# Loading v together with the cast of q and k in an attention and feed-forward kernel, with measured DMA times in its build-time plan

## The chip, the cores and the metric

One core of a Trainium2 chip. The metric is the device time of one execution in microseconds (us), the median of several runs. A profile's span (first to last instruction) is about 1.7 us shorter than the time of the same run. A run that lies more than 1.5% above the fastest of its kernel is called slow here and is left out of every ratio. Ratios are the mean time of one kernel's fast runs over the mean of the kernel before's fast runs of the same rounds, so they are not quite the ratios of the medians that are quoted; each comes with a 95% interval.

## The reference, cut to what matters

```python
# q, k, v: (8 batches, 8 heads, 576 positions, 64)
scores = scale * q @ k.T
# heads 0-3: causal band of 32 positions; heads 4-7: every 4th of the last 128
attn = softmax(where(mask[h], scores, -1e9))
x = (attn @ v)  ->  (4608 tokens, 512)
h = x @ w_in                       # 512 -> 2048
out = (h * sigmoid(h)) @ w_out     # 2048 -> 512
```

## The kernel before

Tokens go through the two layers in nine groups of 512. Layer 1 and layer 2 are 1152 matmuls of 128x512 in all. Batches 0 and 1 get q and k transposed by PE. Batches 2 to 7 take another way, all by DMA:

- **cast(b)**: q and k are copied in DRAM from float32 to float16 (`kq_s`), issued by POOL.
- **turn(b)**: four DMA transposes, issued by SP, bring `kq_s` into SBUF as `nat` and `kqT`.
- **v(b)**: three loads of v with a cast, issued by POOL, into `vraw` and `vp` (two buffers).
- Scores, exp, mask, AV product; x goes to DRAM (`x_s`) by four stores on SP's queue, and one more DMA transpose on SP's queue brings group b back as `xA` or `xR`.

Every engine's queue runs in order. What order the instructions stand in is decided while the program is built, by a small plan in the Python code: it keeps a clock for PE, holds expected durations for everything else, and always picks a step that it believes to be ready. If a date in the plan is too early, the engine stands before a semaphore on the chip, with useful work behind it in its queue.

```python
    class Plan:
        def push(self, step, gen, ready):
            self.now = ready
            ...eng, us = next(gen)...            # runs the code up to the next yield
        def flush(self):
            while self.heap and self.heap[0][0] <= self.t:
                ready, _, step, gen, eng, us = heapq.heappop(self.heap)
                if eng == "DMA":
                    self.push(step, gen, ready + us)
                    continue
    ...
    def count(key, n, then):                     # an event that waits for n others
        counts[key] = counts.get(key, 0) + 1
        if counts[key] == n:
            then()

    def turn_gen(b):
        issue_turn(b)
        yield "DMA", 9.0
        count(("L", b), 3 if b >= 2 * PEB else 2, lambda: start_loads(b))   # PEB = 2

    def loads_gen(b):
        for i in range(2):    # POOL waits here for the transposes of turn(b)
            nc.gpsimd.tensor_copy(fence[:, i : i + 1], kqTs[b % 2][:, i, 1, HN * M - 1 :])
        if b >= 2 * PEB:      # ... and here for the x transpose of group b - 2
            nc.gpsimd.tensor_copy(fence[:, 2:3], x_of(b - 2)[:, HP - 1, GT - 1 :])
        issue_v(b)
        if b + 1 < B:
            issue_cast(b + 1)
        yield "DMA", 7.0
        v_in[b].done = plan.now
        yield "DMA", 6.0
        if b + 1 < B:
            count(("T", b + 1), 2, lambda: start_turn(b + 1))

    def first_cast():                            # cast(2) is issued in the prologue
        yield "DMA", 52.0
        count(("T", PEB), 2, lambda: start_turn(PEB))
```

`turn(b)` waits for two events: cast(b) has landed, and the scores of batch b-2 are placed. `loads(b)` waits for turn(b), for the AV products of batch b-2 and, from batch 4 on, for group b-2.

The softmax here doesn't subtract the row's maximum and nothing guards it: scores larger than these inputs give would overflow.

## Time and profile before

| | before |
|---|---|
| time, median of 3 runs | 371.25 us |
| span of the profiled run | 368.1 us |
| PE busy | 307.8 us, 84% |
| granted TensorE clock, mean | 0.94 |

The first page of the profile, of before. The line PE gives the busy tenths in 40 equal slices of the span (9.2 us each), PEclk the granted clock, DMA the busy share of the 16 DMA engines.

```profile
span 368.1 us, 5678 instructions
PE   0588999299933999499808999999999999999995
PEclk9999999779975999879957999999999999999999
DMA  8999998999995997999998964127100100100112
```

PE is dense from about 195 us on. Before that, and after the start, there are four dents (66, 104, 151 and 182 us), each with a lower granted clock in it or right behind it, while the DMA engines are busy. The three longest of PE's waits, of before (us in total, times, longest):

```profile
PE h L638 <- DVE gT L649: 13.0, 4, 12.0
PE av_p L472 <- DMA vp<-in_v_dram: 12.7, 2, 7.0
PE h L638 <- DMA xA<-x_s: 12.5, 1, 12.5
```

PE's instructions in order of time show where they are. The columns are start, duration, engine, line, tiles, form, count, and in brackets the idle time before and what ended it:

```profile
65.81 0.35 PE L436 MATMUL s<-nat 64*128 64x96 f16 x8
73.14 0.38 PE L472 MATMUL av_p<-vp,probs 128*128 128x65 f16 x4 [6.98 <-DMA vp<-in_v_dram]
73.33 1.90 PE L666 MATMUL y<-w_out,gT 128*128 128x512 f16 x4
...
103.96 0.28 PE L472 MATMUL av_p<-vp,probs 128*128 128x65 f16 x4
116.73 1.89 PE L638 MATMUL h<-xA,w_in 128*128 128x512 f16 x4 [12.48 <-DMA xA<-x_s]
...
157.17 0.38 PE L472 MATMUL av_p<-vp,probs 128*128 128x65 f16 x4 [5.67 <-DMA vp<-in_v_dram]
...
194.37 1.86 PE L638 MATMUL h<-xR,w_in 128*128 128x512 f16 x4 [12.01 <-DVE gT L649]
```

The first line pair: the scores of batch 2 could run, the AV product right behind them found no v, and layer 2 (`y<-w_out`), which needed nothing, stood in the queue behind it. Afterwards four layer matmuls take 1.90 us instead of about 1.03: the granted clock is 0.50 from 73.1 to 79.1 us. This is called the cold clock below.

POOL and SP in order of time, of before, show one cycle: cast and v issued together, the turn (SP), the fences behind it, the next v.

```profile
66.05 0.80 POOL L118 DMA_DIRECT2D kq_s<-in_k_dram  x1
66.83 0.78 POOL L118 DMA_DIRECT2D kq_s<-in_q_dram  x1
85.74 0.19 POOL L306 COPY fence<-kqT 128x1 f16<-128x1 f16 x1 [17.98 <-DMA kqT<-kq_s]
86.90 0.19 POOL L306 COPY fence<-kqT 128x1 f16<-128x1 f16 x1 [0.97 <-DMA kqT<-kq_s]
87.45 1.34 POOL L141 DMA_DIRECT2D vraw<-in_v_dram  x2 [0.37 <-issue]
```

```profile
75.98 5.84 SPq L131 DMA_TRANSPOSE nat<-kq_s  x2
81.87 2.95 SPq L135 DMA_TRANSPOSE kqT<-kq_s  x2
84.93 1.02 SPq L490 DMA_DIRECT2D x_s<-oP  x2
```

Cast 3 was through at 75.98, when the transposes of turn 3 started. They had landed at 86.9, and only then did v of batch 3 leave. SP was taken up for 8.8 us with issuing them, and a store stood behind them.

### The profile page before, as it was taken

What the parts mean: (1) busy time and instruction counts of PE and PEld (TensorE: products, weight loads), DVE (VectorE), ACT (ScalarE), POOL (GpSimd) and SP (SyncE); (2) the same over time, 40 slices, a digit from 0 to 9 for tenths busy, and PEclk for the clock granted to TensorE, in tenths of its full rate; (3) what the DMA queues carried; (4) which work ended last, traced back from release to release, by engine and by line L of the source; (5) the groups of instructions that cost most, each with busy time, mean ns of one, the idle gap of its engine ahead of it and who ended that gap; (6) DMA issues with size and microseconds to landing.
All of it is one profiled execution on the core that took longest, in us unless ns stands there. A gap on an engine that the chain in (4) does not pass through costs nothing.

```text
span 368.1 us, 5678 instructions
## 1 busy us (share of the span) xinstructions
PE 307.8 (84%) x2200; PEld 149.1 (41%) x2200; DVE 198.8 (54%) x477; ACT 153.8 (42%) x258; POOL 48.9 (13%) x80
## 2 busy tenths in 40 slices
PE   0588999299933999499808999999999999999995
PEld 0563545144411444244303444544444444444442
DVE  5694779268940887369404785585345245245200
ACT  1554772036621554435303545445345245245211
POOL 8634001305002200400400300000000000000000
PEclk9999999779975999879957999999999999999999
DMA  8999998999995997999998964127100100100112
GB/s 111 189 203 201 191 199 160 160 214 159 192 195 118 190 241 175 149 190 209 144 216 188 150 89 103 47 90 129 61 28 28 59 28 28 59 29 28 59 62 81
DMA packets 115899, 47.42 MB, mean 129 GB/s; under 512 B 82592, under 2 KB 111264, under 8 KB 115872
## 3 DMA queue, kind: packets, MB, share of 16 engines
q0 software_dynamic: 47152, 19.92, 44.0%
q1 hardware_dynamic: 63536, 17.70, 25.7%
q10 hardware_dynamic: 5184, 9.44, 7.0%
q8 instruction: 17, 0.28, 0.3%
q14 instruction: 10, 0.08, 0.1%
HBM read 39.84 MB, written 20.05 MB: 163 GB/s over the span
## 4 chain that ended last, share of the span: by engine, by line
PE 64%; DMA 22%; POOL 4%; DVE 3%; SPq 2%; issue 2%; ACT 2%; ACTq 0%; POOLq 0%
PE y L666 30%; PE h L638 29%; DMA vp<-in_v_dram 4%; DMA w_out<-in_moe_w_out_dram 4%; DMA xR<-x_s 3%; DMA w_in<-in_moe_w_in_dram 3%; DMA kq_s<-in_k_dram 2%; PE s L436 2%; DMA x_s<-oD 2%; SPq L131 1%; PE av_p L472 1%; DMA nat<-kq_s 1%; POOL vraw L141 1%; PE av_d L472 1%; DMA xA<-x_s 1%
## 5 line engine op out<-in xcount | busy, mean ns | idle before, releaser
L649 DVE SCALAR_TENSOR_TENSOR gT<-th,h 128x512 f16<-128x512 f32 x144 | 97.9, 683 | 86.2 <-ACT th L647 86.0
L666 PE MATMUL y<-w_out,gT 128*128 128x512 f16 x576 | 141.4, 386 | 0.8 <-ACT ob L677 0.7
L647 ACT ACTIVATE th<-h 128x512 f32<-128x512 f32 x144 | 85.9, 597 | 115.4 <-PE h L638 94.3
L638 PE MATMUL h<-xR,w_in 128*128 128x512 f16 x384 | 93.8, 384 | 12.0 <-DVE gT L649 12.0
L638 PEld LDWEIGHTS <-w_in 128*128 128x128 f16 x576 | 54.8, 100 | 89.5 <-issue 22.6
L666 PEld LDWEIGHTS <-gT 128*128 128x128 f16 x576 | 54.5, 99 | 62.2 <-issue 4.3
L638 PE MATMUL h<-xA,w_in 128*128 128x512 f16 x192 | 52.5, 406 | 14.3 <-DMA xA<-x_s 12.5
L677 ACT ACTIVATE ob<-y 128x512 f32<-128x512 f32 x36 | 21.5, 597 | 61.4 <-PE y L666 61.4
L444 ACT ACTIVATE probs<-s 128x768 f16<-128x768 f32 (+2 forms) x45 | 36.4, 810 | 17.6 <-PE s L436 15.5
L472 PEld LDWEIGHTS <-probs 128*128 128x128 f16 x448 | 23.6, 103 | 27.6 <-issue 13.3
L476 DVE TENSOR_TENSOR oD<-av_d,rcps 72x256 f16<-72x256 f32 x64 | 26.9, 420 | 2.2
L472 PE MATMUL av_p<-vp,probs 128*128 128x65 f16 x192 | 13.5, 204 | 14.2 <-DMA vp<-in_v_dram 12.7
L475 DVE RECIPROCAL rcps<-av_p 96x4 f32<-96x4 f32 x48 | 8.3, 173 | 26.2 <-PE av_p L472 26.0
L476 DVE TENSOR_TENSOR oP<-av_p,rcps 96x256 f16<-96x256 f32 x48 | 20.2, 420 | 1.7
L475 DVE RECIPROCAL rcps<-av_d 72x4 f32<-72x4 f32 x64 | 10.9, 171 | 15.7 <-PE av_d L472 15.7
L306 POOL COPY fence<-kqT 128x1 f16<-128x1 f16 x12 | 2.6, 220 | 120.6 <-DMA kqT<-kq_s 120.6
L472 PE MATMUL av_d<-vd,probs 128*128 128x65 f16 x256 | 16.0, 200 | 0.7 <-DVE xA L541 0.3
L451 DVE TENSOR_TENSOR probs<-probs,mask_d 128x864 f16<-128x864 f16 (+1 forms) x24 | 13.2, 550 | 2.7 <-ACT probs L444 2.5
L451 DVE TENSOR_TENSOR probs<-probs,mask_p 128x768 f16<-128x768 f16 x24 | 13.2, 552 | 1.6 <-ACT probs L444 1.4
L406 PE MATMUL td<-ident,nat 96*128 96x96 f16 x48 | 4.3, 242 | 11.1 <-DMA nat<-in_k_dram 6.9
L155 POOL DMA_DIRECT2D vp<-in_v_dram x8 | 11.5, 1439 | 2.2 <-DMA nat<-in_q_dram 2.1
L141 POOL DMA_DIRECT2D vraw<-in_v_dram x16 | 10.8, 677 | 4.3 <-issue 2.0
(62 smaller groups left out, 116.7 us busy)
## 6 DMA issues: line engine op xcount, KB each, us to landing
out_dram<-ob ACTq DMA_DIRECT2D x36, 256.0 KB, 2.4
kq_s<-in_k_dram POOLq DMA_DIRECT2D x6, 576.0 KB, 9.3
kq_s<-in_q_dram POOLq DMA_DIRECT2D x6, 576.0 KB, 11.7
vp<-in_v_dram POOLq DMA_DIRECT2D x7, 384.0 KB, 7.7
w_in<-in_moe_w_in_dram POOLq DMA_DIRECT2D x4, 512.0 KB, 12.0
w_out<-in_moe_w_out_dram POOLq DMA_DIRECT2D x4, 512.0 KB, 16.5
vraw<-in_v_dram POOLq DMA_DIRECT2D x8, 224.0 KB, 5.2
x_s<-oP SPq DMA_DIRECT2D x12, 144.0 KB, 2.2
```

Of the source, the lines that this page charges most:

```text
L141: nc.gpsimd.dma_start(out=vraw[p0 : p0 + m1 - m0, ab].rearrange("p h r d -> p h (r d)"), in_=src[m0:m1],)
L155: nc.gpsimd.dma_start(out=vp[:, j0:, :D], in_=win)
L444: nc.scalar.activation(p2, both[:, :, :n], AF.Exp, scale=scale)
L451: nc.vector.tensor_tensor(p2, p2, mk, ALU.mult)
L472: nc.tensor.matmul(a[:, i, : D + 1], lhs(i), rhs(i), start=True, stop=True)
L475: nc.vector.reciprocal(rcp[:n], a[:n, :, D : D + 1])
L476: nc.vector.tensor_tensor(o, a[:n, :, :D], rcp[:n, :, None].broadcast_to([n, HN, D]), ALU.mult)
L638: nc.tensor.matmul(h, w_in16[:, c, f * P : (f + 1) * P], x_g[:, c], start=(c == 0), stop=(c == HP - 1),)
L647: nc.scalar.activation(th, h, AF.Tanh, scale=0.5)
L649: nc.vector.scalar_tensor_tensor(gTs[g][:, f], th, 1.0, h, ALU.add, ALU.mult)
L666: nc.tensor.matmul(y, gTs[g][:, f, tb * P : (tb + 1) * P], w_out16[:, f], start=(f == 0), stop=(f == NFF - 1),)
L677: nc.scalar.activation(ob, y, AF.Copy, scale=0.5)
```

## The change

The intent: v of a batch leaves together with the cast of the same batch, before its turn, so that v is long there when the scores are done; one batch per cycle; and the plan gets the durations that were measured (turn 12.5 us, v 9.0, cast 4.5 more). The first cast moves out of the prologue, behind v(2). Cut to its core:

```diff
-    issue_cast(2)
...
     def turn_gen(b):
         issue_turn(b)
-        yield "DMA", 9.0
-        count(("L", b), 3 if b >= 2 * PEB else 2, lambda: start_loads(b))
+        yield "DMA", 12.5
+        if b + 1 < B:
+            count(("L", b + 1), loads_need(b + 1), lambda: start_loads(b + 1))
+
+    def loads_need(b):
+        return 3 if b >= 2 * PEB else 2 if b > PEB else 1
...
     def loads_gen(b):
-        for i in range(2):
-            nc.gpsimd.tensor_copy(fence[:, i : i + 1], kqTs[b % 2][:, i, 1, HN * M - 1 :])
+        if b > PEB:
+            for i in range(2):
+                nc.gpsimd.tensor_copy(fence[:, i : i + 1], kqTs[(b - 1) % 2][:, i, 1, HN * M - 1 :])
...
         issue_v(b)
-        if b + 1 < B:
-            issue_cast(b + 1)
-        yield "DMA", 7.0
+        issue_cast(b)
+        yield "DMA", max(9.0, 52.0 - plan.now)
         v_in[b].done = plan.now
-        yield "DMA", 6.0
-        if b + 1 < B:
-            count(("T", b + 1), 2, lambda: start_turn(b + 1))
+        yield "DMA", 4.5
+        count(("T", b), 2, lambda: start_turn(b))
...
-    def first_cast():
-        yield "DMA", 52.0
-        count(("T", PEB), 2, lambda: start_turn(PEB))
```

The two other places that count `("L", b + 2)` now use `loads_need(b + 2)`.

More of the change, by code (lines that the diff above doesn't have):

```diff
@@ L333, in group_gen @@
         if g == b and b + 2 < B:
-            count(("L", b + 2), 3, lambda: start_loads(b + 2))
+            count(("L", b + 2), loads_need(b + 2), lambda: start_loads(b + 2))
     def stored(b):
@@ L622, in attention @@
                             lambda: count(
-                                ("L", b + 2), 3 if b >= PEB else 2, lambda: start_loads(b + 2)
+                                ("L", b + 2), loads_need(b + 2), lambda: start_loads(b + 2)
                             )
@@ L692, in layer2 @@
         return steps
-    plan.push(Step(None, 0.0), first_cast(), 0.0)
     att = []
```

## The prediction

> **What bounds it.** PE is busy 84% of the 368.1 us span, but by ten-microsecond windows it is dense only from 201 us on. Before that (PE lines and waits in order of time) it stands still four times after the first layer-1 matmul at 29.4 us: 66–73 us (7.0, for vp of batch 2), 104–117 (12.5, xA of token group 2), 151–157 (5.7, vp of batch 5), 182–194 (12.0; behind it an ACT queue that waits for the DMA transposes of batch 7). That is 37 us. After each stop the matmuls take twice as long for a while (1.71 instead of 0.86 us for four). The Trainium skill, "TensorE: Matmul & The Clock Gate", Part 1, says an idle PE drops to half rate until about 3.4 us of activity; the trace agrees: some 3 us a stop, 11 in all.
>
> Floor from the trace: 1152 layer matmuls at 0.2165 us = 249, attention of seven batches near 5 us each = 35, 3 for batch 1's transposes, 29.4 lead, 3.5 tail: 320 us. So about 48 us are stops and cold clock.
>
> **Why it stops.** Queues are in order, the order is fixed at build time. The plan counts 9.0 us for a turn (four transposes); the trace shows 10.9 to 12.7. It counts 7 us for v, the trace 9.7. And v(b) is issued only after turn(b) has landed (POOL's fence waits 120.6 us for kqT), so the AV product behind the scores finds no v.
>
> **The change** adds and removes no work: same bytes, a few fences less. cast(2) moves behind v(2). v(b) leaves with cast(b), before turn(b). In the trace v+cast takes 11.0 to 12.7 us to land, the turn as above; the new plan has 13.5 and 12.5, slightly conservative, as it should be.
>
> Estimated course: v(2)+cast(2) land at 54 us (50.2 now, plus 0.77 MB at about 195 GB/s), turn(2) at 66, v(2) long there. No vp stop. Attention takes some 22 us a batch, so batch 2 is stored by 93 and group 2 turned by 98 instead of 116.7. Groups 0 and 1 with attention keep PE busy until about 98: little of the 12.5 us stop stays.
>
> **Its cost.** cast(b) and turn(b) now wait for group b-2 as well. The loop over two batches is load 12 + turn 11.5 + attention 22 + store behind SP's turn issue (up to 9) + x transpose 6 = 55 to 60 us, so 28 to 30 per group, like today's spacing (28 to 31). PE needs about 32 per group (27.7 layers + 5 attention), so it should just stay fed, with small stops from SP's blocked stores, which the plan doesn't know.
>
> **Prediction.** Floor 320, plus 5 to 14 for remaining stops and cold clock, plus 2 from span to time: 334 us (10% less), range 318 to 354. Chances: faster by over 2% 0.88, within 2% 0.07, slower 0.05.
>
> **Signs that it is right:** vp no longer among PE's waits in mid-span; group 2's first layer-1 matmul near 98 us; idle PE after 29 us below 15 us; granted clock mean about 0.97; PE work unchanged; last x transpose earlier than now (255 us).
>
> **What would make it wrong:** cast(2) landing after 60 us behind v(1) and w_out; a loop longer than 33 us per group, so that PE starves at every group; ACT's output DMAs again held behind late transposes; or scores placed early, so that stops move from vp to the transposes.

## The result, and the profile after

| | before | after |
|---|---|---|
| median of 4 runs | 370.88 us | 340.75 us (336.27 to 341.09) |
| ratio, 95% interval | 1 | 0.9154 (0.9073 to 0.9235) |
| span of the profiled run | 368.1 us | 339.4 us |
| PE busy | 307.8 us | 304.1 us |
| mean granted clock | 0.94 | 0.985 |

The first page, of after, and PE's longest waits, of after (those of the first 29 us are left out):

```profile
span 339.4 us, 5670 instructions
PE   0678998999999883999999999599999999999995
PEclk9999999999999997999999999879999999999999
DMA  8999999899759995995699989972260100200121
```

```profile
PE h L636 <- DMA xR<-x_s: 6.0, 1, 6.0
PE s L434 <- DMA nat<-kq_s: 3.6, 1, 3.6
PE h L636 <- DVE gT L647: 2.6, 5, 0.8
```

The vp wait is gone, and of four dents two are left, near 130 and 215 us. PE in order of time, of after:

```profile
73.62 0.35 PE L434 MATMUL s<-nat 64*128 64x96 f16 x8
...
103.92 1.02 PE L636 MATMUL h<-xA,w_in 128*128 128x512 f16 x4
...
124.63 1.89 PE L636 MATMUL h<-xA,w_in 128*128 128x512 f16 x8
132.49 3.28 PE L636 MATMUL h<-xR,w_in 128*128 128x512 f16 x8 [5.97 <-DMA xR<-x_s]
...
218.38 0.51 PE L434 MATMUL s<-nat 64*128 64x96 f16 x8 [3.59 <-DMA nat<-kq_s]
```

Batch 2's first scores stand at 73.6 us, and PE runs through the place where it stood for v. Group 2 starts at 103.9 instead of 116.7. Then group 3 is late (132.5). SP in order of time, of after, shows what it waited behind:

```profile
109.25 0.86 SPq L507 DMA_DIRECT2D x_s<-oD  x1
115.03 6.91 SPq L131 DMA_TRANSPOSE nat<-kq_s  x2
122.04 2.72 SPq L135 DMA_TRANSPOSE kqT<-kq_s  x2
124.85 0.85 SPq L507 DMA_DIRECT2D x_s<-oD  x1
127.77 2.53 SPq L326 DMA_TRANSPOSE xR<-x_s  x1
```

The last store of batch 3 had its data at 114.47 us (DVE wrote `oD` there) and was issued at 124.85, behind the four transposes of turn 4. The x transpose of group 3 could only follow.

**Reading the plan against the chip.** The plan's own dates can be printed while the program is built, and each step's date compared with the start of the same matmuls in the trace: the 2200 PE matmuls of the trace answer the plan's steps one to one. The difference is the chip's lag behind the plan. It grows mainly where PE stands still or runs cold (a few lines, in us):

```
                           before              after
                           plan  chip  lag     plan  chip  lag
group 0, layer 1           26.1  29.4   3.2    26.1  28.8   2.7
batch 2, first scores      58.0  62.8   4.9    69.3  73.6   4.4
batch 2, first AV product  60.9  73.1  12.3    72.6  76.9   4.2
group 2, layer 1           90.0 116.7  26.8   100.3 103.9   3.6
group 3, layer 1          121.9 150.2  28.3   123.2 132.5   9.3
batch 5, first AV product 123.1 157.2  34.0   149.8 160.5  10.7
batch 6, first scores     147.4 196.2  48.8   184.6 195.3  10.8
batch 7, first scores     178.5 228.3  49.7   204.1 218.4  14.3
group 8, layer 1          273.7 322.5  48.9   277.3 293.8  16.5
```

So the new plan itself ends 3.6 us later than the old one (319.0 against 315.4 us). All the gain, and more, is that the chip keeps up with it: the lag fell from 48.9 to 16.5 us. In every kernel of this case the span was the plan's end plus the lag at group 8 plus 3.8 to 4.0 us. (The plan's end is its last step's end. The expectations of runs 1 to 8 below give the start of that step, 0.9 us earlier.)

The printed dates also show *what* was false in the old plan. It held turn 2 for landed at 28.8 us and v of batch 2 at 30.9; on the chip it was 62.8 and 73.0. No duration of 9 or 7 us explains that. The cause is `count`. The code after a `yield` runs as soon as the wait *begins*, with the clock of the event set to its *end* (cast 2: 52 us). `count` drops that date: `then()` starts at the date of whoever is counted last, and for turn 2 that was the placing of the scores of batch 0, at 19.8 us. The changed kernel has the same `count`, but there loads(2) waits for one event alone, and for turn 2 the late event happens to be counted last. Its plan for batch 2 is therefore true (69.0); for loads(3) it is false again (59.4, while the turn that it waits for ends at 69.0 in the same plan).

### The profile page after: what moved, and what is told of

Same layout as the page of the kernel before. It is cut to its first block, busy times and chain, and to the rows that moved or that the text cites. A ratio compares the mean times of both kernels' runs of the same rounds, so it can differ in the third digit from the quotient of the medians.

```text
span 339.4 us, 5670 instructions
## 1 busy us (share of the span) xinstructions
PE 304.1 (90%) x2200; PEld 147.2 (43%) x2200; DVE 200.3 (59%) x477; ACT 154.2 (45%) x258; POOL 49.5 (15%) x78
## 4 chain that ended last, share of the span: by engine, by line
PE 80%; DVE 7%; DMA 6%; ACT 4%; issue 1%; POOL 1%; ACTq 0%; SPq 0%; POOLq 0%
PE y L664 36%; PE h L636 35%; PE s L434 3%; PE av_d L470 2%; DMA nat<-in_q_dram 2%; DVE gT L647 2%; PE av_p L470 2%; ACT th L645 2%; ACT ob L675 1%; DMA xR<-x_s 1%; DMA nat<-kq_s 1%; DVE oD L474 1%; DVE oP L474 1%; PE td L404 1%; DVE probs L449 1%
## 5 line engine op out<-in xcount | busy, mean ns | idle before, releaser
L636 PE MATMUL h<-xR,w_in 128*128 128x512 f16 x384 | 95.7, 388 | 6.1 <-DMA xR<-x_s 6.0
L664 PEld LDWEIGHTS <-gT 128*128 128x128 f16 x576 | 53.2, 98 | 60.8 <-issue 3.0
L636 PE MATMUL h<-xA,w_in 128*128 128x512 f16 x192 | 48.5, 390 | 2.8 <-DVE gT L647 2.6
L442 ACT ACTIVATE probs<-s 128x768 f16<-128x768 f32 (+2 forms) x45 | 36.4, 810 | 22.3 <-PE s L434 19.8
L141 POOL DMA_DIRECT2D vraw<-in_v_dram x16 | 10.8, 677 | 5.1 <-DMA nat<-in_k_dram 2.4
## 6 DMA issues: line engine op xcount, KB each, us to landing
kq_s<-in_q_dram POOLq DMA_DIRECT2D x6, 576.0 KB, 12.5
w_out<-in_moe_w_out_dram POOLq DMA_DIRECT2D x4, 512.0 KB, 16.6
```

Of the source, the lines that this page charges most:

```text
L141: nc.gpsimd.dma_start(out=vraw[p0 : p0 + m1 - m0, ab].rearrange("p h r d -> p h (r d)"), in_=src[m0:m1],)
L442: nc.scalar.activation(p2, both[:, :, :n], AF.Exp, scale=scale)
L636: nc.tensor.matmul(h, w_in16[:, c, f * P : (f + 1) * P], x_g[:, c], start=(c == 0), stop=(c == HP - 1),)
L664: nc.tensor.matmul(y, gTs[g][:, f, tb * P : (tb + 1) * P], w_out16[:, f], start=(f == 0), stop=(f == NFF - 1),)
```

## The experiments

Three theories of the gain: **A**, v leaves before the turn (the order); **A'**, the measured durations; **B**, a plan whose dates are true, whatever the order. Runs 1 to 4 ran on one chip. "Before" was 370.7 us there. The changed kernel was not run again beside the experiments; it is compared with them through its own ratio to before (0.9154), which comes from an earlier session. One run of four was slow in each of runs 3, 8 and 11, two of four in runs 10 and 12.

### 1. The durations alone

```diff
 (kernel before)
-        yield "DMA", 9.0
+        yield "DMA", 12.5
...
-        yield "DMA", 7.0
+        yield "DMA", 9.0
         v_in[b].done = plan.now
-        yield "DMA", 6.0
+        yield "DMA", 4.5
```

> The kernel before with the change's measured times alone (turn 12.5, v 9.0, cast 4.5 us); the order of loads as before. Printed at build, this plan ends layer 2 at 314.5 us and still holds v of batch 2 for landed at 32.9 us (the chip: 73), because an event that waits for several things takes the time of whichever is counted last. Theory A (what pays is that v leaves before the turn): 365 to 372 us, as before. Theory A' (what pays is the measured times): about 341. Theory B (what pays is a plan whose arrivals are true, and the counting is what made it false): 360 to 372, with the vp stop near 66 us still there, some 7 us.

Measured: 365.68 us, ratio 0.9881 (0.9816 to 0.9946). Two of PE's waits of this run:

```profile
PE h L638 <- DMA xA<-x_s: 14.0, 1, 14.0
PE av_p L472 <- DMA vp<-in_v_dram: 11.8, 2, 6.2
```

The stops for v and for group 2 are about as long as before. A' falls. What shrank is the fourth stop: PE's wait `h <- DVE gT`, 13.0 us before, is 5.5 us here.

### 2. The order alone

```diff
 (changed kernel)
-        yield "DMA", 12.5
+        yield "DMA", 9.0
...
-        yield "DMA", max(9.0, 52.0 - plan.now)
+        yield "DMA", max(7.0, 46.0 - plan.now)
         v_in[b].done = plan.now
-        yield "DMA", 4.5
+        yield "DMA", 6.0
```

> The changed order of loads with the old times (turn 9.0, v 7.0, cast 6.0 us; first v at 46, first cast at 52). Theory A (the order pays): 341 to 348 us, no stop for vp. Theory A' (the times pay): 360 to 372. Theory B (true arrivals pay): in between, 345 to 355: the new order has fewer false arrivals, but each turn is planned 2 to 3 us too early, so stops move to the transposes and to the x groups.

Measured: 352.1 us, ratio 0.949 (0.9435 to 0.9545). The stop moved, as B said:

```profile
PE s L434 <- DMA nat<-kq_s: 16.7, 3, 10.8
```

No wait for vp, but 16.7 us for transposes that the plan holds for done after 9 us. (They took 10.9 to 12.7 us in before, so the 9 alone does not explain the longest stop, 10.8 us for batch 7; its other part was not traced.) The order brings 5.1%, and with the durations 8.5%. This edit of the order also changes what `count` gets wrong (turn 2 is dated 61.0 us here, 28.8 in before), so the 5.1% is not the worth of the order alone.

### 3 and 4. The old order with honest counting

```diff
 (kernel before; run 4 has run 1's durations too)
+    latest = {}
     def count(key, n, then):
         counts[key] = counts.get(key, 0) + 1
+        latest[key] = max(latest.get(key, 0.0), plan.now)
         if counts[key] == n:
+            plan.now = latest[key]
             then()
```

> The kernel before with one edit: an event that waits for several things starts at the latest of them, not at the one counted last. Old order, old times. The plan then has turn 2 landed at 61 us, v of batch 2 at 68 (before: 28.8 and 30.9), and ends at 315.0. Theory A (order of v): 365 to 372. Theory A' (the times): 365 to 372. Theory B (true arrivals): 340 to 352, no 7 us stop for vp of batch 2, small stops of 2 to 4 us per batch, since a turn is still planned 2 us too short.

Measured (run 3): 357.43 us, ratio 0.9616 (0.9542 to 0.9691). Faster, but less than B said: the plan gives a cycle of 22 us (turns 2 to 7 landed at 61, 83, 105 and so on), where a cycle of before took 24 us at best, and two stops for vp come back, for batches 5 and 7:

```profile
PE av_p L476 <- DMA vp<-in_v_dram: 17.2, 2, 8.8
```

> The kernel before with the old order of loads, the honest count and the measured times (turn 12.5, v 9.0, cast 4.5). Its plan ends at 319.5 us, against 318.2 for the changed kernel. Theory A (v before the turn is what pays): 360 us or more. Theory B (a true plan pays, in either order): 326 to 340 us, lag of the chip behind the plan below 17 us at the end (before: 49, after: 16.5).

Measured (run 4): 346.54 us, ratio 0.9355 (0.9307 to 0.9402), lag 20.1 us. A falls as the whole explanation: v still leaves after the turn, and 6.5 of the 8.5% are there. B promised a little too much (326 to 340 us, lag below 17). Two of PE's waits of run 4:

```profile
PE h L642 <- DMA xA<-x_s: 5.0, 1, 5.0
PE av_p L476 <- DMA vp<-in_v_dram: 4.0, 1, 4.0
```

The durations were worth 1.2% beside a false count and 2.6 points (0.9616 to 0.9355) beside a true one.

### 5 to 8. What is left: SP's queue, or false dates?

Theory **C**: stores of x stand behind transposes in SP's queue. Theory **D**: the plan's dates for batches 3, 5 and 7 are still false by the count. All four ran on one chip (before: 369.7 us).

```diff
 5 (changed kernel), stores from ACT's queue; both places
-                nc.sync.dma_start(          # x_s <- oP, x_s <- oD
+                nc.scalar.dma_start(
 6 (changed kernel), honest count: the edit of run 3
 7 (run 6), the turn as four steps of the plan
-        issue_turn(b)
-        yield "DMA", 12.5
+        for part in issue_turn(b):          # yields 3.2, 3.2, 1.4, 1.4 after its transposes
+            yield "DMA", part
+        yield "DMA", 3.3
 8 (run 7), and the stores from ACT's queue
```

> The changed kernel with the 24 stores of x issued from ACT's queue instead of SP's; plan unchanged. In the changed kernel SP holds the last store of batch 3 back behind the four transposes of turn 4 (store ready near 114 us, issued 124.85), and the same with batches 5 and 6. Theory C (SP's in-order queue is what is left to gain): group 3 comes about 3 us earlier (its x transpose still stands behind turn 4), as does group 5; 334 to 338 us. Theory D (what is left is that the plan's arrivals for batches 3, 5 and 7 are up to 10 us too early, because of the counting): 339 to 342, nothing gained.

> The changed kernel with the honest count (an event that waits for several things starts at the latest). Its plan ends later, 322.0 us against 318.2. Theory C: SP still holds stores behind transposes: 339 to 344. Theory D (false arrivals are what is left): lag behind the plan at the end falls from 16.5 to 7 to 11 us, the stops for group 3 (6.0 us) and for batch 7's transposes (3.6) go, 333 to 338 us.

> The kernel of the honest count, and a turn issued as four steps in the plan, so that stores and x transposes may stand between its four transposes in SP's queue. The plan's times are the same as with the honest count alone (322.0 us). Theory C: 3 to 6 us faster than the honest count alone. Theory D alone: the same as the honest count alone within 1.5 us, since there the stores are planned after the turn anyway.

> Honest count, turn in four steps and stores from ACT's queue together. If C and D both hold it is the fastest: 328 to 335 us. If ACT waits for the stores' data or for a semaphore of a transpose, it stops instead, as it did near 182 us in the kernel before: 340 us or more.

| run | median us | ratio (95%) | plan's end | lag |
|---|---|---|---|---|
| after | 340.75 | 0.9154 (0.9073–0.9235) | 319.0 | 16.5 |
| 5 stores on ACT | 344.71 | 0.9322 (0.9262–0.9382) | 319.0 | 21.7 |
| 6 honest count | 342.31 | 0.9241 (0.9179–0.9304) | 322.8 | 13.6 |
| 7 and turn in four | 341.25 | 0.921 (0.9145–0.9275) | 322.8 | 15.0 |
| 8 and stores on ACT | 344.87 | 0.9293 (0.9217–0.9369) | 322.8 | 16.6 |

None is faster than the changed kernel, and neither C nor D gets what it promised. Honest counting did lower the lag, by 2.9 us, and made the plan 3.8 us longer. Turning in four halved group 3's stop (2.6 instead of 5.6 us in run 6) and gave it back as a stop of 3.8 us for batch 7's transposes, which now share SP's queue with the stores. With the stores on ACT, group 3 waits 3.4 us (run 5) or nothing (run 8), but ACT, which empties PSUM for PE, is held up: in run 8 its queue stood 13.5 us for `oD`, the data of the stores, and 4.7 us for the transposes `nat<-kq_s` (neither is among its waits in after), as the expectation had warned. PE's two longest waits after the start, of run 8:

```profile
PE h L643 <- DVE gT L654: 10.4, 13, 3.1
PE y L671 <- ACT ob L682: 6.0, 6, 2.2
```

In the profile after these were 2.6 and 1.9 us.

### 9 to 12. The dates of batch 2, the gate of the loads, and a plan without slack

Theory **E**: group 2 came at 103.9 instead of the predicted 98 because the plan dates batch 2's scores late, and all else hangs on it. Theory **F**: the stops only move. One chip (before: 370.8 us).

```diff
  9 (changed kernel)                       10: the same on run 6
-        yield "DMA", max(9.0, 52.0 - plan.now)
+        yield "DMA", max(9.0, 46.0 - plan.now)
 11 (run 10), loads no longer wait for group b-2
-        return 3 if b >= 2 * PEB else 2 if b > PEB else 1
+        return 2 if b > PEB else 1
...
-        if b >= 2 * PEB:
-            nc.gpsimd.tensor_copy(fence[:, 2:3], x_of(b - 2)[:, HP - 1, GT - 1 :])
...
-        b = need[g]
-        if g == b and b + 2 < B:
-            count(("L", b + 2), loads_need(b + 2), lambda: start_loads(b + 2))
 12 (run 7), first v at 46, cast 3.0 instead of 4.5, last yield of the turn 2.1 instead of 3.3
```

> The changed kernel with one number of its plan changed: the first v is expected at 46 us instead of 52 (so cast 2 at 50.5, turn 2 landed at 63 instead of 69). In the changed kernel turn 2 has landed at 66.6 us on the chip, but its scores stand at 73.6, because the plan put them late; group 2 came at 102.4 instead of the predicted 98. Theory E (group 2's late arrival is the mis-sized term, and every later group hangs on it): first scores of batch 2 near 67 us, group 2 near 97, and the whole 4 to 7 us faster than the changed kernel, 333 to 337 us. Theory F (the stops of the chip behind the plan are what is left; they only move): group 2 earlier, but 338 to 343 us.

> The same with the honest count. Plan end 317.9 us (honest count with 52: 322.8; the changed kernel: 319.0). Every span so far was the plan's end plus the final lag of the chip behind it plus 3.9 us. Theory E: lag stays at 13 to 14 as with the honest count, so a span of 335 to 336, time 335 to 338. Theory F: lag grows by what the plan gained, 340 to 343.

> The one before, without the wait of the loads of batch b for the x transpose of group b-2 (it is no data dependence). It tests the predicted cost of the change: that v, cast and turn of a batch now hang on group b-2. If that loop limits the groups, batches 4 to 7 are turned 5 to 10 us earlier, the groups come every 26 us or less, and it is 3 to 8 us faster than the run with the gate. If loads then collide with the stores and transposes of x (DMA saturated), groups come as late as before or later: equal or slower.

> Honest count, first v at 46, cast 3.0 after v instead of 4.5, turn in four steps with 11.3 us in all instead of 12.5: the durations as the trace has them, without slack. Plan end 317.2 us. If slack in the plan costs what it adds, 333 to 337 us. If a plan without slack is caught out by every late landing (as the run with the changed order and the old times was: lag 30.8), 340 to 348 us.

| run | median us | ratio (95%) | plan's end | lag |
|---|---|---|---|---|
| 9 first v at 46 | 341.53 | 0.9239 (0.9197–0.9282) | 317.5 | 17.1 |
| 10 honest, 46 | 340.99 | 0.9143 (0.9082–0.9203) | 317.9 | 16.0 |
| 11 no gate | 354.77 | 0.9549 (0.9475–0.9623) | 318.1 | 34.6 (slow run) |
| 12 no slack, in four | 343.6 | 0.9209 (0.9138–0.928) | 317.2 | 19.7 |

Run 9 is the direct test of E, and E falls. Group 2 starts 5.3 us earlier, at 98.6 us, as had been predicted; group 3 only 1.4 us earlier, and PE's wait for it grew from 6.0 to 8.7 us. PE and then SP in order of time, of run 9:

```profile
131.10 3.37 PE L636 MATMUL h<-xR,w_in 128*128 128x512 f16 x8 [8.65 <-DMA xR<-x_s]
```

```profile
112.16 7.33 SPq L131 DMA_TRANSPOSE nat<-kq_s  x2
119.60 2.94 SPq L135 DMA_TRANSPOSE kqT<-kq_s  x2
122.63 0.85 SPq L507 DMA_DIRECT2D x_s<-oD  x1
126.20 2.77 SPq L326 DMA_TRANSPOSE xR<-x_s  x1
```

The store of batch 3 was ready at 111.3 us (DVE) and again waited for turn 4 to be issued. Run 12, where stores may pass, waits only 0.9 us for groups, but 11.3 us for transposes.

Run 11 says the opposite of what it was made for: without the gate it is slower than run 10 in fast runs (350.75, 354.33 and 355.21 us against 337.22 and 339.58). So the gate, which is no data dependence, pays; why was not shown. One reading is that it keeps the loads apart from the stores and transposes of x. That transfers meet on the DMA engines there fits what the Trainium skill says ("DMA: Bandwidth & Descriptors", "Issuing engines are not separate DMA queues": transfers of all issuing engines run on the same 16 DMA engines and interleave), but the meeting itself was not measured. A rival is SP's queue: other dates also change which stores stand behind which transposes. Its profile fell on the one slow run, so its lines are not shown.

No version is clearly faster than the changed kernel; run 10 (0.9143) ties with it (0.9154).

## Why the prediction was right or wrong

The time (334 predicted, 340.75 measured) lies in the range and the direction is right. Point by point:

- **"PE stands still four times ... 37 us": right; "some 3 us a stop" of cold clock, "11 in all": somewhat high.** After the four stops of before PE worked 6.0, 3.3, 3.8 and 4.1 us at a granted clock of 0.50. Half of that, 8.6 us, is an estimate of the loss. The lag table books 44 us between batch 2's first scores and batch 6's, about these 37 us and the cold matmuls. The Trainium skill's statement on the idle PE ("TensorE: Matmul & The Clock Gate", Part 1) agrees with the trace after as well: behind the 6.0 us stop eight matmuls took 3.28 us instead of 1.89.
- **"No vp stop": right.** vp is not among PE's waits after.
- **"The plan counts 9.0 us for a turn ... 7 us for v" as a reason: a part, and small alone.** Those durations alone are worth 1.2% (run 1); once the dates are otherwise nearer the truth, they are worth 2.6 points (run 3 to run 4). The larger false dates came from `count`, which the prediction had not read closely: it reads as if an event started at the latest of its conditions, and it starts at the last one counted. The printed plan shows it (28.8 against 62.8 us), run 3 repairs it and nothing else, and gains 3.8%. The change met this by luck: nothing in the prediction aims at it, but in the new plan the late event of turn 2 happens to be counted last, so the worst of the false dates went away.
- **"And v(b) is issued only after turn(b) has landed ... finds no v": not the reason as it stands.** In run 4 v still leaves after the turn, and most of the gain is there. What matters most is whether the plan knows it. With honest counting and the measured durations in both, the new order is worth 0.9355 against 0.9241 (run 6, on another chip), about one point. No run has the new order with dates as false as those of before.
- **"Group 2 turned by 98": off, 102.4 (POOL's fence for `xA`), first matmul 103.9.** Turn 2 was done as predicted (66.6 us against 66), but the plan dated it 69.0 and the chip lagged 4.4 us behind the plan, so the scores stood at 73.6. This term is 6 us, about the size of the whole miss (6.8 us). But run 9 shows that it was not what the total hung on: with group 2 at 98.6 the time stayed.
- **"28 to 30 per group ... should just stay fed": too small.** Groups 2 to 5 came 30.1, 34.1 and 29.6 us apart (POOL's fences at 102.4, 132.6, 166.7, 196.3). The "store behind SP's turn issue (up to 9)" was seen: 10.4 us for batch 3. That is the term that was mis-sized: "5 to 14 for remaining stops and cold clock" over the floor of 320 us came out as 19.4 us of span. The two stops that are left (6.0 us for group 3, 3.6 for the transposes of batch 7) and the cold clock behind them (8.5 us at 0.50, so some 4 us lost, an estimate) make 14 of these; the rest was not added up.
- **Signs:** idle PE after 29 us was 20.5 us (310.6 us less 290.1 busy; 45.1 in before), not below 15. The mean clock was 0.985 (0.97 predicted). The same 2200 matmuls. The last x transposes were issued from 244.1 us on, instead of 250.6.

What is left (lag 16.5 us, and some 11 us of gaps between PE's steps after 25 us in the plan itself) stayed open: C, D and E each name a wait that is really there, and removing it lets another grow, the group's, the transposes' or ACT's. The runs support one supply chain for group 3 and later (load, turn, attention, store, x transpose) that PE waits for at one place or another; they do not show its shortest form. One more stop of before has to be explained, the 12.0 us near 182 us. PE waited for DVE, DVE for ACT, and ACT's queue stood before an output store until transposes of turn 7 had landed. SP and ACT in order of time, of before:

```profile
187.40 5.12 SPq L131 DMA_TRANSPOSE nat<-kq_s  x2
192.56 0.34 ACTq L678 DMA_DIRECT2D out_dram<-ob  x1
193.00 1.08 ACT L647 ACTIVATE th<-h 128x512 f32<-128x512 f32 x2 [12.60 <-DMA nat<-kq_s]
```

The store needs no data of the transposes. But in the packed trace the DMAs of SP and ACT share eight completion semaphores (the counters that tell that a transfer has landed; 111 to 118), and this store has the same one, 116, as the transpose that SP issued at 187.40. That transpose counted up 116 for the last time at 192.48, ACT's wait for 116 ended at 192.50, and the store left at 192.56. Which DMA follows which on a semaphore was settled at build time, and the plan of before held turn 7 for landed at 151.1. So this stop, too, goes with a date that was far too early; in run 3, with honest counting, the wait `h <- DVE gT` is 1.0 us in all. No run changed the semaphores alone. In after the stop does not occur; ACT had short ones of the same kind in run 6 (2.2 us) and run 8 (4.7 us).

## What to carry to other kernels

Where the order of instructions is planned at build time, print the plan's dates and lay them beside the trace: the places where the lag grows are where to look for false dates, and one false rule can do more than all durations together (3.8% against 1.2% here, each alone). Before a gain is put down to a new order of transfers, run the old order with a true plan. And when a stop is repaired and the time stays, look for the stop that grew.

## What the Trainium skill lacked or had wrong

- "DMA: Bandwidth & Descriptors", "Issuing engines are not separate DMA queues", says that the sequencer's time to start a DMA "is usually small relative to the DMA itself". This does not hold for the DMA transposes here: the four of a turn took up SP's queue for 8.8 us of the 10.9 us from first issue to last landing (turn 3 of before), and a store behind such a turn waited 10.4 us (after).
- The same section says that issuing from several engines saves sequencer time only. What the section lacks is the price: 24 stores moved from SP to ACT gained nothing (0.9322 against 0.9154 for the same plan, in different sessions; 0.9293 against 0.921 for run 8 against run 7 on one chip, where the intervals overlap), with PE's waits for ACT's PSUM evictions (`y <- ACT ob`) grown from 1.9 us (after) to 4.8 us (run 5).
